# An attention and expert-routing kernel with its chunk loads relaid to 112 and 128 rows, quarter-tile scores and token-major outputs

## The chip, the cores and the metric

The kernel runs on one core of one Trainium2 chip. The metric is the device time in microseconds of one execution; what is shown is the median of three runs.

## The reference

An mLSTM (linear attention with exponential gates) feeds a mixture of experts that keeps the 80 best tokens of each expert.

```python
def _attn_ref(q, k, v, i_gate, f_gate, o_gate):      # B, H, S, D = 4, 8, 768, 40
    for t in range(S):
        m_new = np.maximum(f_gate[:, :, t] + m, i_gate[:, :, t])
        f_stab = np.exp(f_gate[:, :, t] + m - m_new)
        i_stab = np.exp(i_gate[:, :, t] - m_new)
        m = m_new
        C = f_stab * C + i_stab * outer(v[t], k[t])   # per batch and head, 40 x 40
        n = f_stab * n + i_stab * k[t]
        denom = np.maximum(np.abs(n @ q[t]), 1.0)
        y[t] = sigmoid(o_gate[t]) * (C @ q[t]) / denom

def _moe_ref(x, w_gate, w1, w2, capacity):            # 3072 tokens x 320, 8 experts, 1024 hidden
    expert_idx = argmax(x @ w_gate);  gate_w = softmax(x @ w_gate)[expert_idx]
    for e in range(E):
        tok_idx = tokens of e, at most the `capacity` (80) of largest gate_w
        out[tok_idx] = gate_w[tok_idx] * (relu(x[tok_idx] @ w1[e]) @ w2[e])
```

Tokens that no expert keeps stay zero in `out`.

## The kernel before, in words

The sequence is cut into 12 chunks of 64 steps (`NC`, `T`). The 32 pairs of batch and head are 16 groups of two; each chunk is done in two half chunks of eight groups, so there are 24 steps `i` (`NHS`), with chunk `c = i // 2` and half `hb = i % 2`. Within a chunk the recurrence is a masked score matrix; between chunks a 40 x 41 state is carried (`cs`, with a copy `cb` in the layout that the matmul wants). The stages of a step:

- `s_arg` (L371, L373): a matmul of `lh` and `rc` makes the logarithms of the decay in PSUM, and ACT's exp writes `w`. `lh` and `rc` hold gate sums that go through a DRAM tile (`d2`: `store_d2`, `load_lh`, `load_rc`).
- `s_s` (L398): scores S = K Q, eight matmuls that are each two records in the profile; `s_p` (L404): DVE multiplies S with `w` into `p`; `s_kw` (L388): POOL scales the keys.
- `s_int` (L424): the part from the carried state, in `hib`; `s_pv` (L412): `p` times V, in `h`; `s_st` (L433): the state update, in `cps`.
- `s_post` (L441 to L456): DVE puts the parts together, makes the reciprocal `rd` of the denominator and the product `u` with the output gate; POOL multiplies `u` and `rd` into `xn`.
- `s_state` (L483 to L493): DVE adds the update to the decayed state, and ACT copies it to `cb` in four pieces of 40 x 164. In three of the steps (`OFF`) DVE and POOL copy.
- `s_tp`, `s_xt` (L508, L523): PE transposes the finished 128 x 320 tile, ACT copies it out of PSUM; `s_z`, `s_lg` (L531, L545, L546) make the gating logits of a chunk by matmul, copy, transpose and reduction; `s_gate` picks the expert; `s_cmp` and `s_cnt` count gate values over thresholds; `s_xd` (L540) stores the finished chunk to DRAM.

Each chunk comes in by six loads from SP's queue: two of `qk` (40 rows each), two of `q2` (the queries in a second layout, 40 rows each) and two of `kv` (64 rows each), into two buffers (`NV = 2`). The rows of a buffer that no load fills are set to zero once, before the loop (`zeros`, `zero_v`).

The order on each engine is written out by hand. `PRE` lists the operations before the loop, `BODY` the stages of one step (run for i = 2 to 21), `TAIL` those after it; all DMAs in these lists are issued by SP in that order, so that a DMA that waits holds up those behind it.

In the loop SP also loads the output gates (`og` into `xn`), the weights of the first expert pair (`b_w`, four parts), and writes zeros over the whole output in four DMAs (`b_zero`, steps 9, 10, 17, 21).

After the loop and its tail, routing finds for each expert the 80 largest gates by three rounds of comparisons (L908 to L969), eight indirect DMAs gather the tokens, and the experts follow in four pairs (`f_h`, `f_o`), with weights streamed in behind; indirect DMAs scatter the result over the zeroed output.

Of the kernel before, what the change touches and what calls it, by code (L numbers as in the profile page):

```python
# [9 lines left out]
F32 = mybir.dt.float32  # L10
# [9 lines left out]
NP = 4  # L20
# [5 lines left out]
VN, KN = G16 * V1, G16 * D  # L26
E = 8
# [46 lines left out]
def tile_mlstm_moe(ctx, tc, cap, qk_d, q2_d, kv0_d, kv1_d, og_d, if_d, cst_d, cs2_d, zr_d, wz_d, w1_d, w2_d, out_d, dbg=None):  # L74
# [72 lines left out]
    zt = cp.tile([128, 480], F32, name="zt")  # L147
# [36 lines left out]
    A.activation(ez, zb[0:1, 0:1], AF.Exp)  # L184
# [144 lines left out]
    def store_d2(c0, c1):  # L329
        s, e = c0 * T, c1 * T  # L330
        SP.dma_start(d2[:, :, :, :, s:e].rearrange("k a g h t -> (g h) (k a) t"),
                     lb[:, :, :, s:e].rearrange("r k a t -> r (k a) t"))
# [58 lines left out]
    def s_s(i):  # L391
        c, hb = divmod(i, 2)
        qk = qk_b[c % NV]
        sp = ps.tile([128, 4, 2, T], F32, tag="s", name=f"s{i}")
        for q in range(4):
            for y in range(2):
                g = 8 * hb + 2 * q + y
                TE.matmul(sp[64 * y:64 * y + 64, q], lhsT=qk[:, 1, g], rhs=qk[:, 0:3:2, g], start=True, stop=True)  # L398
        pp = wk.tile([128, 8, T], F32, tag="p", name=f"p{i}")
        st["p", i] = (pp, sp.rearrange("r q x t -> r (q x) t"))  # L400

    def s_p(i):
        pp, sp = st["p", i]
        V.tensor_tensor(pp, sp, st.pop(("w", i)), ALU.mult)  # L404

    def s_pv(i):
        c, hb = divmod(i, 2)
        pp, _ = st.pop(("p", i))
        hp = (ps if i == NHS - 1 else ps1).tile([128, 4, 2, V1], F32, tag="s" if i == NHS - 1 else "h", name=f"h{i}")
        for p in range(8):  # L410
            r0 = 64 * (p % 2)
            TE.matmul(hp[r0:r0 + 64, p // 2], lhsT=pp[:, p], rhs=vb[c % NV][:, :, 8 * hb + p], start=True, stop=True)  # L412
        st["h", i] = hp

    def s_int(i):
# [3 lines left out]
        hi = ps1.tile([128, 512], F32, tag="ar", name="hil")[:, 0:8 * V1].rearrange("r (q y v) -> r q y v", y=2, v=V1) if i == NHS - 1 else hiv  # L419
        st["hi", i] = hi  # L420
        for p in range(8):
            g = 8 * hb + p
            r0 = 64 * (p % 2)
            TE.matmul(hi[r0:r0 + 64, p // 2], lhsT=q2_b[c % NV][:, g], rhs=cb[:, :, g], start=True, stop=True)  # L424
# [784 lines left out]
```

## Time and profile before

| | |
|---|---|
| runs | 265.21, 265.52, 266.19 us; median 265.52 |
| profiled execution | span 271.7 us (first to last instruction); no other time of it is given |
| PE, DVE, ACT, POOL busy in it | 222.0, 134.1, 92.3, 106.2 us |
| moved by DMA | 55.68 MB, mean 205 GB/s |
| mean granted TensorE clock | 0.858 |

An engine's busy time is a sum over stages with different limits. A row of a window gives for one stretch the busy time of PE, PEld (weight loads), DVE, ACT and POOL with the number of instructions, the granted TensorE clock as a share, the mean busy share of the 16 DMA engines, and GB/s. A row of the timeline gives start, length, engine, line, operation, output and inputs, and in brackets how long the engine was idle before and what ended that. KB are 1024 bytes, MB and GB powers of ten.

### The profile page before, as it was taken

What the parts mean: (1) busy time and instruction counts of PE and PEld (TensorE: products, weight loads), DVE (VectorE), ACT (ScalarE), POOL (GpSimd) and SP (SyncE); (2) the same over time, 40 slices, a digit from 0 to 9 for tenths busy, and PEclk for the clock granted to TensorE, in tenths of its full rate; (3) what the DMA queues carried; (4) which work ended last, traced back from release to release, by engine and by line L of the source; (5) the groups of instructions that cost most, each with busy time, mean ns of one, the idle gap of its engine ahead of it and who ended that gap; (6) DMA issues with size and microseconds to landing.
All of it is one profiled execution on the core that took longest, in us unless ns stands there. A gap on an engine that the chain in (4) does not pass through costs nothing. (4 is left out here: it accounts for less than half of the span.)

```text
span 271.7 us, 7189 instructions
## 1 busy us (share of the span) xinstructions
PE 222.0 (82%) x2938; PEld 164.7 (61%) x2938; DVE 134.1 (49%) x393; ACT 92.3 (34%) x215; POOL 106.2 (39%) x195
## 2 busy tenths in 40 slices
PE   6795999239746999799493889887897999999992
PEld 2364877128534977587382676656455896489640
DVE  8975989806741579789444488533700000100010
ACT  5465466537432955244333333200000121013100
POOL 9761766445545265666440831300047000111021
PEclk9999599759995799899869599865657699999998
DMA  5986479889889978979999965960012999980010
GB/s 125 192 223 173 156 195 276 170 195 224 229 201 281 231 237 232 215 211 186 331 208 215 257 193 135 421 291 0 2 32 76 364 420 420 422 372 24 0 39 23
DMA packets 21337, 55.68 MB, mean 205 GB/s; under 512 B 5000, under 2 KB 14024, under 8 KB 18552
## 3 DMA queue, kind: packets, MB, share of 16 engines
q1 hardware_dynamic: 20488, 53.33, 67.6%
q0 software_dynamic: 672, 1.64, 2.0%
q8 instruction: 23, 0.38, 0.6%
q10 hardware_dynamic: 144, 0.26, 0.3%
q14 instruction: 10, 0.08, 0.1%
HBM read 46.26 MB, written 9.12 MB: 204 GB/s over the span
## 5 line engine op out<-in xcount | busy, mean ns | idle before, releaser
L388 POOL TENSOR_TENSOR kw<-kv,w 128x320 f32<-128x320 f32 x22 | 16.7, 759 | 50.1 <-DMA kv<-in_kv 39.2
L398 PE MATMUL s<-qk 128*64 128x128 f32 x384 | 33.1, 327 | 2.2 <-DMA qk<-in_qk 0.8
L398 PEld LDWEIGHTS s<-qk 128*64 128x64 f32 x384 | 26.4, 166 | 10.9 <-issue 7.1
L493 ACT COPY cb<-cs 40x164 f32<-40x164 f32 x76 | 25.1, 330 | 11.0 <-DVE cs L483 8.9
L1025 PE MATMUL hp<-cx,w 128*64 128x80 f32 x512 | 25.6, 243 | 2.0 <-issue 1.6
L412 PE MATMUL h<-kv,p 128*64 128x82 f32 x384 | 20.2, 251 | 7.8 <-DMA kv<-in_kv 7.8
L1064 POOL DMA_INDIRECT out<-ob,iqi x6 | 5.9, 978 | 52.7 <-DVE ob L1061 36.0
L1057 PE MATMUL op<-w,ht 128*64 128x320 f32 (+1 forms) x256 | 26.4, 433 | 0.0
L1025 PEld LDWEIGHTS hp<-cx,w 128*64 128x64 f32 x512 | 24.3, 146 | 2.5 <-issue 1.8
L371 PE MATMUL ar<-rc,lh 118*128 118x512 bf16 x22 | 10.0, 456 | 18.2 <-DMA qk<-in_qk 9.2
L456 POOL TENSOR_TENSOR xn<-u,rd 128x320 f32<-128x320 f32 x23 | 17.3, 755 | 15.4 <-DVE u L455 14.3
L412 PEld LDWEIGHTS h<-kv,p 128*64 128x64 f32 x384 | 17.7, 150 | 8.8 <-issue 6.1
L441 DVE TENSOR_TENSOR hs<-hib,gn 128x328 f32<-128x328 f32 x21 | 10.3, 493 | 21.7 <-PE hib L424 21.7
L1057 PEld LDWEIGHTS op<-w,ht 128*64 128x64 f32 (+1 forms) x256 | 12.6, 117 | 12.8 <-issue 5.3
L373 ACT ACTIVATE w<-ar 128x512 f32<-128x512 f32 x22 | 13.1, 596 | 20.8 <-PE ar L371 20.0
L1061 DVE TENSOR_SCALAR ob<-op,iq 128x320 f32<-128x320 f32 (+1 forms) x6 | 3.1, 523 | 33.1 <-PE op L1057 33.1
L972 POOL DMA_INDIRECT xg<-xd,idx x8 | 7.9, 985 | 29.6 <-DVE gi L980 27.5
L523 ACT COPY xt<-tp 128x384 f32<-128x384 f32 x20 | 9.5, 479 | 29.4 <-PE tp L508 29.3
L424 PE MATMUL hib<-cb,q 128*64 128x82 f32 x336 | 17.9, 254 | 1.8 <-DMA q<-in_q 1.5
L433 PE MATMUL cps<-kv,kw 128*40 128x82 f32 x352 | 18.9, 255 | 0.0
L1044 ACT ACTIVATE ht<-hp 128x320 f32<-128x320 f32 x16 | 7.0, 437 | 34.5 <-PE hp L1025 34.5
L424 PEld LDWEIGHTS hib<-cb,q 128*64 128x64 f32 x336 | 16.4, 153 | 2.9 <-DVE p L404 1.1
(215 smaller groups left out, 415.7 us busy)
## 6 DMA issues: line engine op xcount, KB each, us to landing
w<-in_w SPq DMA_DIRECT2D x14, 1280.0 KB
kv<-in_kv SPq DMA_DIRECT2D x24, 324.0 KB
qk<-in_qk SPq DMA_DIRECT2D x24, 320.0 KB
xd<-xn SPq DMA_DIRECT2D x24, 160.0 KB
out<-zt SPq DMA_DIRECT2D x4, 960.0 KB
q<-in_q SPq DMA_DIRECT2D x22, 160.0 KB
xn<-in_og SPq DMA_DIRECT2D x9, 320.0 KB
w<-in_w SPq DMA_DIRECT2D x4, 640.0 KB
```

The source lines that it names most:

```text
L371: TE.matmul(ar, lhsT=lh[:, c].rearrange("r h t -> r (h t)"), rhs=rc[c // 2 % NRC][:, gs_(i), c % 2, :], start=True, stop=True)
L373: A.activation(w, ar, AF.Exp)
L388: P.tensor_tensor(kw, kn_b[c % NV][:, gs_(i)], st["w", i][:, :, T - 1:T].broadcast_to([128, 8, D]), ALU.mult)
L398: TE.matmul(sp[64 * y:64 * y + 64, q], lhsT=qk[:, 1, g], rhs=qk[:, 0:3:2, g], start=True, stop=True)
L412: TE.matmul(hp[r0:r0 + 64, p // 2], lhsT=pp[:, p], rhs=vb[c % NV][:, :, 8 * hb + p], start=True, stop=True)
L424: TE.matmul(hi[r0:r0 + 64, p // 2], lhsT=q2_b[c % NV][:, g], rhs=cb[:, :, g], start=True, stop=True)
L433: TE.matmul(cpv[r0:r0 + 40, p // 2], lhsT=kw[:, p], rhs=vb[c % NV][:, :, 8 * hb + p], start=True, stop=True)
L441: V.tensor_tensor(hs, st.pop(("hi", i)), gn[:, c, gs].rearrange("r (q a) -> r q a", a=2).unsqueeze(3).broadcast_to([128, 4, 2, V1]), ALU.mult)
L456: P.tensor_tensor(xn[:, i], u, rd.broadcast_to([128, 8, D]), ALU.mult)
L493: A.copy(dst, src)
L1025: TE.matmul(out, lhsT=w[:, k, c0:c0 + 64], rhs=rhs, start=start, stop=stop)
L1057: TE.matmul(o[gw * j:gw * j + m, 0:DM], lhsT=hts[p][:, f, a, t0:t0 + m], rhs=w[:, a, f], start=(f == 0), stop=(f == 7), tile_position=(0, ...
```

## The change

- *Loads.* One `qk` tile of 112 rows (q and k of one half of the groups in rows 0 to 39, of the other in rows 64 to 103, zeros between them written on the host) and one `kv` tile of 128 rows (values in a block layout with their zeros, and keys). `q2` and the zero fills go. Three buffers.
- *Scores.* S by 16 matmuls on quarters of the array (40 rows in, 64 out, 64 columns) into one PSUM tile of two banks.
- *Outputs.* Rows of `xn` are tokens with all heads in order; the store `xd` has rows of 1280 B instead of 640 B. `w_gate` and `w1` keep their order.
- *Logits.* `s_z` writes the logits of each half chunk to PSUM directly; the copy `zs`, its transpose and the reduction go.
- *Post.* One fused step for the absolute value, `u` on POOL, and the product with the clipped reciprocal on DVE (`s_fin`). The copies to `cb` are two of 40 x 328, always on ACT.
- *Order.* `gt` and `cst` are loaded in two parts; the first round trip of the gates through DRAM is issued by ACT; the output is zeroed after the loop, behind two weight tiles; the first weight tile is loaded in steps 18 to 21 instead of 15 on; sigmoids in four groups instead of three; gates chosen at other steps.

```diff
-BODY = "tab pr0 cmp s zero int pv tp st load xt xd cg p w post arg0 pr1 cnt pg z state d2 arg1 sig lh og lg"
+BODY = "tab pr0 cmp s int pv tp st load xt xd cg p w post arg0 pr1 cnt pg z state fin d2 arg1 sig lh og"
-PRE = "qb msk qa lq0 ad0 zv0 zc mkb wm lk0 al0 fl lo p0 p0 qc0 p0 ...
+PRE = "lq0 lgt lk0 lo0 lcb lq1 lk1 lo1 msk zc mkb wm ad0 al0 fl p0 p0 p0 p0 p1 p0 sig a0 brc p1 s0 ...
-    SP.dma_start(gt, if_d)
+    SP.dma_start(gt[:, :, 0:2 * T], if_d[:, :, 0:2 * T])
-    A.dma_start(cst, cst_d)
+    A.dma_start(cst[:, 0:CST_A], cst_d[:, 0:CST_A])
-    NV = 2
-    qk_b = [cp.tile([128, 3, G16, T], F32, name=f"qk{i}") for i in range(NV)]
-    q2_b = [cp.tile([128, G16, T], F32, name=f"q2{i}") for i in range(NV)]
-    kv_b = [cp.tile([128, 2, VN + KN], F32, name=f"kv{i}") for i in range(NV)]
+    NV = 3
+    qk_b = [cp.tile([QR, 2, G16, T], F32, name=f"qk{i}") for i in range(NV)]
+    kv_b = [cp.tile([128, KVN], F32, name=f"kv{i}") for i in range(NV)]
+    sps = ps1.tile([128, 2, 2, 4, T], F32, tag="s", name="sps")
     def load_qk(c):
-        SP.dma_start(qk_b[j][0:40, 0:2], qk_d[c, 0])
-        SP.dma_start(qk_b[j][64:104, 1:3], qk_d[c, 1])
+        SP.dma_start(qk_b[c % NV], qk_d[c])
     def load_kv(c):
-        SP.dma_start(kv_b[j][0:64, 0], kv0_d[c])
-        SP.dma_start(kv_b[j][64:128].rearrange("r y n -> r (y n)")[:, VN:2 * VN + KN], kv1_d[c])
+        SP.dma_start(kv_b[c % NV], kv_d[c])
     def s_s(i):
-        sp = ps.tile([128, 4, 2, T], F32, tag="s", name=f"s{i}")
+        sp = sps[:, :, hb]
         for q in range(4):
             for y in range(2):
-                TE.matmul(sp[64 * y:64 * y + 64, q], lhsT=qk[:, 1, g], rhs=qk[:, 0:3:2, g], start=True, stop=True)
+                for x in range(2):
+                    g = 8 * hb + 2 * q + y
+                    r = slice(64 * x, 64 * x + D)
+                    TE.matmul(sp[64 * y:64 * y + 64, x, q], lhsT=qk[r, 1, g], rhs=qk[r, 0, g], start=True, stop=True)
     def s_int(i):
-            TE.matmul(hi[r0:r0 + 64, p // 2], lhsT=q2_b[c % NV][:, g], rhs=cb[:, :, g], start=True, stop=True)
+                    TE.matmul(hi[64 * r:64 * r + 64, 2 * a:2 * a + 2, y], lhsT=qk_b[c % NV][0:104, 0, g], rhs=cb[:, g], start=True, stop=True)
     def s_post(i):
-        V.tensor_scalar(rd, hv[:, :, D:V1], -1.0, 1.0, ALU.mult, ALU.max)
-        V.tensor_tensor(rd, hv[:, :, D:V1], rd, ALU.max)
+        V.scalar_tensor_tensor(rd, hv[:, :, D:V1], -1.0, hv[:, :, D:V1], ALU.mult, ALU.max)
+        P.tensor_tensor(u, hv[:, :, 0:D], xn[:, i], ALU.mult)
         V.reciprocal(rd, rd)
-        (V if i < UV else P).tensor_tensor(u, hv[:, :, 0:D], xn[:, i], ALU.mult)
-        P.tensor_tensor(xn[:, i], u, rd.broadcast_to([128, 8, D]), ALU.mult)
+    def s_fin(i):
+        V.scalar_tensor_tensor(xn[:, i], rd.broadcast_to([128, 8, D]), 1.0, u, ALU.min, ALU.mult)
     def s_state(i):
-        for x in range(2):
-            for y in range(2):
-                ...
         for x in range(2):
+            r = slice(64 * x, 64 * x + D)
+            A.copy(cb[r, gs, x], cs[r, 4 * hb:4 * hb + 4].rearrange("r q y v -> r (q y) v"))
+    def s_z(i):
+        lgp = lga[:, i] if i < LG else st["lgb"][:, i - LG]
+        for k in range(3):
+            for r in range(2):
+                TE.matmul(lgp[64 * r:64 * r + 64], lhsT=xt[:, k, 64 * r:64 * r + 64], rhs=wz[:, k], start=(k == 0), stop=(k == 2))
-        sd1=lambda: store_d2(1, 2), lh1=lambda: load_lh(1, 2),
+        sd1=lambda: store_d2(1, 2, A), lh1=lambda: load_lh(1, 2, A),
-    def b_zero(i): ...
     for p_, kind, k in ((wp, 0, 1), (wq, 1, 0)):
         run(load_w(p_, kind, k))
+    for k in range(4):
+        SP.dma_start(out_d.rearrange("(p r) d -> p (r d)", p=128)[:, 1920 * k:1920 * (k + 1)].rearrange("p (r n) -> p r n", n=480),
+                     zt.unsqueeze(1).broadcast_to([128, 4, 480]))
```

More of the change, by code (lines that the diff above doesn't have):

```diff
@@ L192, in warmc @@
         for _ in range(n):
-            TE.matmul(cps, lhsT=zb[:, 0:128], rhs=zb, start=True, stop=True)
+            TE.matmul(sps[:, 0].rearrange("r h q t -> r (h q t)"), lhsT=zb[:, 0:128], rhs=zb, start=True, stop=True)
     def c2(name, rows=128):
@@ L509, in s_tp @@
         st["tp", i] = tp
[L510 removed]
     def s_xt(i):
[L513 to L516 removed]
+        xt = wk.tile([128, 3, 128], F32, tag="xt", name=f"xt{i}")
+        st["xt", i] = xt
         tp = st.pop(("tp", i))
[L518 removed]
+        if i == NHS - 1:
             V.tensor_copy(xt[:, 0:XL], tp[:, 0:XL])
[L520 to L523 removed]
@@ L525, in s_z @@
-    def s_z(c):
-        st["zx"] = st["x"]
-        xt = st.pop(("xt", c))
-        for k in (0, 1, 2):
-            for x in range(2):
-                j = 2 * x + (k == 1)
-                TE.matmul(st["zx"][32 * j:32 * j + 32], lhsT=wz[:, x, k], rhs=xt[:, k, :, 64 * x:64 * x + 64],
-                          start=(k < 2), stop=(k > 0), tile_position=(0, 32 * j))
-        zs = wk.tile([128, 128], F32, tag="zs", name=f"zs{c}")
-        A.copy(zs, st["zx"])
-        st["zs", c] = zs
-    def s_xd(c):
-        i = 2 * c + 1
-        for eo in range(2):
-            SP.dma_start(
-                xd.rearrange("(b s) e f -> s b e f", b=B)[c * T:(c + 1) * T, :, eo],
-                xn[64 * eo:64 * eo + 64, i - 1:i + 1].rearrange("t h (b p) d -> t (h b) (p d)", b=2))
@@ L544, in s_lg @@
-    def s_lg(c):
-        TE.transpose(st["zx"], st.pop(("zs", c)), ident)
-        V.tensor_reduce(lg[:, c].rearrange("r a e -> r (a e)"), st["zx"].rearrange("r (j e) -> r e j", j=4)[:, 0:2 * E], AX.X, ALU.add)
-    def s_gate(c0, c1, lv=None):
+            A.copy(xt[:, XL:3], tp[:, XL:3])
+        else:
+            A.copy(xt, tp)
+    def s_z(i):
+        xt = st.pop(("xt", i))
+        if i == LG:
+            st["lgb"] = ps1.tile([128, 2, E], F32, tag="h", name="lgb")
+        lgp = lga[:, i] if i < LG else st["lgb"][:, i - LG]
+        for k in range(3):
+            for r in range(2):
+                TE.matmul(lgp[64 * r:64 * r + 64], lhsT=xt[:, k, 64 * r:64 * r + 64], rhs=wz[:, k], start=(k == 0), stop=(k == 2))
@@ L549, in s_gate @@
+    def s_xd(c):
+        for r in range(2):
+            SP.dma_start(xd.rearrange("(b r s) f -> r s b f", r=2, s=S)[r, c * T:(c + 1) * T],
+                         xn[64 * r:64 * r + 64, 2 * c:2 * c + 2].rearrange("t b h d -> t b (h d)"))
+    def s_gate(c0, c1):
         n = c1 - c0
         sh = [128, 2 * n, E]
-        lv = lg[:, c0:c1].rearrange("r c a e -> r (c a) e") if lv is None else lv
+        lv = lga[:, 2 * c0:2 * c1] if c1 < NC else st["lgb"]
         gv = gate[:, c0:c1].rearrange("r c a -> r (c a)")
@@ L615, in s_cnt @@
             V.tensor_tensor(ncnt, ncnt, cpc, ALU.subtract)
-    def s_zl(hb):
-        if hb == 0:
-            st["zl"] = ps1.tile([128, 2, E], F32, tag="h", name="zl")
-        xt = st["xt", NC - 1][:, :, hb]
-        for k in (0, 1, 2):
-            for x in range(2):
-                TE.matmul(st["zl"][64 * hb:64 * hb + 64], lhsT=xt[:, k, 64 * x:64 * x + 64],
-                          rhs=wz[:, x, k, 0:2 * E], start=(k == 0 and x == 0), stop=(k == 2 and x == 1))
     def s_sig(i):
@@ L714, in b_xt @@
     def b_xt(i):
-        if i >= 3 and i not in OFF:
+        if i >= 3:
             s_xt(i - 1)
@@ L738, in b_z @@
     def b_z(i):
-        if i >= 3 and i % 2 == 1:
-            s_z((i - 3) // 2)
+        if i == 2:
+            s_z(0)
+        s_z(i - 1)
     def b_cmp(i):
@@ L1158, in by_x @@
         return six(a).transpose(4, 2, 6, 0, 1, 3, 5).reshape(NC, 2, D, G16, T)
-    def by_y(a):
-        return six(a).transpose(4, 3, 6, 0, 1, 2, 5).reshape(NC, 2, D, G16, T)
     def nat(a):
```

268 lines of the change are left out of this document (104 added, 164 removed).

## The prediction

> **What bounds the kernel now.** I read the stages first (windows of the span: busy time of each engine, granted TensorE clock, DMA share, GB/s), cut at the first inter-chunk matmul (29.60), at that of iteration 22, the first after the loop (159.4), at the start of routing (171.4) and at the expert matmuls (207).
>
> ```profile
> 0.00:29.60 29.60, 22.49 (x166) 13.11 (x166) 23.16 (x68) 17.15 (x26) 18.62 (x23) 0.96 0.76 180
> 29.60:159.40 129.80, 100.46 (x1559) 80.85 (x1558) 82.66 (x229) 60.70 (x149) 68.81 (x144) 0.84 0.88 224
> 159.40:171.40 12.00, 10.67 (x151) 7.88 (x150) 9.91 (x47) 5.13 (x16) 3.73 (x7) 1.00 0.58 176
> 171.40:207.00 35.60, 30.79 (x165) 20.28 (x166) 13.33 (x41) 0.39 (x2) 6.58 (x9) 0.66 0.34 132
> ```
>
> The columns are PE, PEld, DVE, ACT, POOL, clock, DMA share, GB/s. The second row is half the span: 20 loop iterations, 6.49 us each. No compute engine fills it (PE 100.5 of 129.8, at a mean clock of 0.84), but the DMA engines are busy 0.88 of it at only 224 GB/s. Next, the waits of that stretch (total, times, longest):
>
> ```profile
> POOL kw L388 <- DMA kv<-in_kv: 36.4, 6, 10.8
> ...
> DVE hs L441 <- PE hib L424: 21.7, 11, 9.1
> ```
>
> Six waits for `kv` stand at the head; the PE and DVE waits behind them are their echo. Then the rate of each kind of transfer, in windows in which nearly nothing else moves (64-row `kv`; 40-row `qk`; zeroing of the output from 128 rows; `xd` stores; 128-row expert weights):
>
> ```profile
> 21.00:23.00 2.00, 1.41 (x34) 1.25 (x31) 1.90 (x10) 1.95 (x5) 0.02 (x1) 1.00 0.59 135
> 28.00:31.80 3.80, 3.80 (x44) 3.22 (x45) 3.77 (x10) 2.24 (x9) 3.38 (x6) 0.50 0.61 213
> 85.50:88.00 2.50, 2.50 (x23) 1.53 (x23) 0.87 (x2) 1.01 (x5) 1.23 (x2) 0.50 1.05 397
> 167.00:168.00 1.00, 1.00 (x21) 0.87 (x20) 0.63 (x5) 0.25 (x2) 0.00 (x0) 1.00 0.94 234
> 223.00:233.00 10.00, 10.00 (x126) 6.74 (x124) 1.11 (x3) 1.31 (x4) 1.01 (x1) 1.00 1.01 420
> ```
>
> Loads of 40 or 64 rows leave 0.4 of the DMA engines idle even alone, and move 135 to 213 GB/s; 128-row transfers fill them and move 397 to 420. So the loop is bound by how its loads are shaped. What would the loop cost without that? The inter-chunk matmuls (16 records an iteration) count iterations:
>
> ```profile
> 29.60:42.90 13.30, 2.10 (x32) 1.79 (x32) 0.82 0.69 183
> 61.60:75.20 13.60, 2.21 (x48) 2.02 (x50) 1.00 0.91 228
> 89.30:108.70 19.40, 3.52 (x64) 3.20 (x64) 0.92 0.86 232
> 116.10:128.85 12.75, 2.21 (x48) 2.04 (x48) 1.00 0.86 195
> ```
>
> The last three hold 3 + 4 + 3 iterations in 45.75 us: 4.58 each, where data are nearly in time. The first two iterations take 13.3, laden with the gate scans. The PE timeline of a quiet iteration shows its pace:
>
> ```profile
> 102.68 0.33 PE L545 MATMUL tp<-cst,zs 128*128 128x128 f32 x1
> 102.94 1.09 PE L398 MATMUL s<-qk 128*64 128x128 f32 x16
> 103.86 0.74 PE L424 MATMUL hib<-cb,q 128*64 128x82 f32 x16
> 104.43 0.74 PE L412 MATMUL h<-kv,p 128*64 128x82 f32 x16
> 105.09 0.55 PE L508 MATMUL tp<-cst,xn 128*128 128x128 f32 x3
> 105.57 0.77 PE L433 MATMUL cps<-kv,kw 128*40 128x82 f32 x16
> 106.27 0.63 PE L531 MATMUL tp<-xt,wz 128*32 128x128 f32 x12
> 106.83 0.39 PE L371 MATMUL ar<-rc,lh 118*128 118x512 bf16 x1
> 107.15 0.44 PE L398 MATMUL s<-qk 128*64 128x128 f32 x4
> ```
>
> From S (102.94) to the next S (107.15) is 4.21 us without a gap: behind the DMA stands PE.
>
> **The change part by part.** The sum is made against the profiled execution (span 271.7; the page gives no other time of it); the median of the runs is 265.52, so 6.2 go off at the end.
>
> ```profile
> kv<-in_kv SPq DMA_DIRECT2D x24, 324.0 KB
> qk<-in_qk SPq DMA_DIRECT2D x24, 320.0 KB
> xd<-xn SPq DMA_DIRECT2D x24, 160.0 KB
> out<-zt SPq DMA_DIRECT2D x4, 960.0 KB
> q<-in_q SPq DMA_DIRECT2D x22, 160.0 KB
> ```
>
> *Loads.* A chunk (two iterations) now takes 2x324 + 2x320 + 2x160 = 1608 KB in six issues. By the shapes in the diff it becomes 128 x 1952 x 4 B = 976 KB of `kv` and 112 x 2048 x 4 B = 896 KB of `qk` in two issues: 1872 KB, 264 more, padding included. At 420 GB/s that is 4.56 us. With 320 KB of `og` at 397 (0.83) and 320 KB of `xd` at 234 (1.40) a chunk costs 6.8 us of transfer in the 9.2 that two iterations take. So DMA drops from the bound to 74%; bounds 6.8 (these rows) and, if the new loads stay at 224 GB/s, 11.5. I take the first, since 128 rows are the shape of the 420 row; 112 rows are nearer to it than to 64. A third buffer lets a load start about 2.5 iterations (11 us) before its first use, against some 5 us of transfer.
>
> *Zeroing.* 4 x 960 KB = 3.93 MB leave the loop: 9.9 us of DMA at 397 GB/s, inside what is counted above. It is queued on SP behind two weight tiles (5.2 MB, 12.5 us at 420) after the loop. The cover is routing: 35.6 us at a DMA share of 0.34, that is 12.1 busy; 22 of 35.6 after. The next SP instruction behind it is the store of the indices, at the end of routing. Cost 0; without the cover, 9.9.
>
> *PE.* S goes from 16 records of 128 columns to 32 of 64 columns on quarter tiles. In the timeline S takes 0.92 start to start (57 ns a record of 128 columns), L424 0.57 (36 ns, 82 columns). Extended to 64 columns: 27 ns, 32 x 27 = 0.87. If four quarters overlap, half of it, 0.43. Unoverlapped small records are these 24, 1.4 us in all, 57 ns each:
>
> ```profile
> L493 ACT COPY cb<-cs 40x164 f32<-40x164 f32 x76 | 25.1, 330 | 11.0 <-DVE cs L483 8.9 <-DVE cs L485 0.6
> ...
> L523 ACT COPY xt<-tp 128x384 f32<-128x384 f32 x20 | 9.5, 479 | 29.4 <-PE tp L508 29.3
> ...
> L623 PE MATMUL zl<-wz,xt 128*64 128x16 f32 x24 | 1.4, 211 | 0.0
> ```
>
> That gives 1.8. I take 0.92, no change; range -0.5 to +0.9 an iteration. S loses its separate PSUM buffers (the halves now share banks): S of i+2 must follow the product `p` of i, which DVE was given an iteration earlier, and 0 is taken for it. The Trainium skill, TensorEngine Tiling (Array Packing), section Performance Considerations, says that a matmul costs some 60 cycles however few its columns are, and that a tiling factor should not be taken from a dimension already small. It also says (Tiling Modes) that a change of tiling mode drains the array. It speaks against quarter tiles: at 2.4 GHz, an estimate of 25 ns x 32 = 0.8 and two drains more an iteration. By it the sum moves by less than 2 us.
>
> Logits change from 12 records every second iteration plus a transpose (0.56 + 0.26 over two, 0.41) to 12 records each iteration, 0.32 to 0.68 by the same two prices: +0.1. Inter-chunk, PV and state matmuls keep count and width.
>
> *ACT, DVE, POOL.* The state copies become 2 of 328 elements for 4 of 164: between the two ACT rows 0.68 ns an element, so 0.44 each, 0.88 for 1.32. The zs copy goes, so ACT gains some 0.5 an iteration, in idle time: 0 on the path. DVE trades `u` for the fused min-multiply (same size) and loses one of two small steps and the logit reduction; POOL trades the `xn` product for `u`. Both stay below PE (82.7 and 68.8 us for 20 iterations now, 4.1 and 3.4 each), so 0. One new order: `xn` now waits for POOL's `u`, then DVE; its reader, the transpose, stands 3 us into the next PE iteration.
>
> Loop: 18 x (4.58 + 0.1) = 84.2, the first two 13.3, rest waits 1.5: 99. It is 129.8 now: -30.8.
>
> *Before the loop.* The zero fills go, the gate inputs and constants are split so the scans start sooner, and the gates' round trip through DRAM goes to ACT's queue:
>
> ```profile
> 5.78 0.28 DVE L297 TENSOR_TENSOR_SCAN m<-gt 32x64 f32<-32x64 f32 x1
> ...
> 12.90 0.34 SPq L331 DMA_DIRECT2D d<-lb  x1
> ...
> 25.76 0.38 PE L371 MATMUL ar<-rc,lh 118*128 118x512 bf16 x1 [2.34 <-DMA rc<-d]
> ```
>
> Store to matmul is 12.9 us, with bulk loads queued between on SP. The scans can start some 3 us sooner, and the trip can shrink by 5 or more; against that, four DMAs are issued by ACT, which stands still until the store has landed, with the first state copies and the exp of iteration 2 behind it (DVE and PE wait for these), and the first sigmoid, ahead of the first exp, now waits for its `og`. SP, rid of them, issues the loads of chunks 2 and 3 sooner. Bounds -9 and +3; I take -6. *Behind the loop:* a few small DVE steps and two transposes of the 0.26 kind less, -0.5 (bounds -1.5, +2). Routing and experts: the same work, 0.
>
> Sum: -30.8 - 6 - 0.5 = -37.3: span 234.4, runs 228.
>
> **The rivals.** *A2, serial quarters:* S costs 1.8 instead of 0.92, 20 x 0.88 = +18 on a loop that PE paces: 246. For it: 57 ns at L623; against: those 24 write one half of the PSUM rows, then the other; S's 32 alternate over four quarters.
>
> *B, the byte rate stays:* the padded loads move no faster than 224 GB/s. Ten chunks of 1872 + 640 KB and a weight tile (2560 KB) are 28.3 MB, 126 us: loop -3.5, with the prologue -6 and -0.5 behind: 255.5. For it: `xd` and 64-row traffic interleave with everything; against: 397 and 420 in two windows. Forecast and B part at 28.3 MB / 99 us = 286 GB/s. The Trainium skill (SBUF — State Buffer, section on door 1, the DMA port swizzle) says that DMA bandwidth depends on how many of 16 ports the rows reach, and that 64 adjoining rows reach half. By that rule 112 and 128 rows are freed, and 4.56 us a chunk holds; the 135 and 213 GB/s rows agree.
>
> *C, nothing moves:* as B, and ACT's wait for the round trip costs the 3 of its bound instead of giving 6: -3.5 + 3 - 0.5 = -1, 264.5. For it: ACT also carries the exps; against: they wait for the same trip today.
>
> *D, slower:* gaps between small matmuls make the granted clock fall to half inside S (0.50 is seen in the 28.0 window), with no quarters overlapping: 32 x 114 ns = 3.65 for S, 7.4 an iteration, loop 18 x 7.4 + 14.8 = 148, +18 - 6.5 = +11.7: 277. It decides from S = 3.0 on (loop 136, then 18 iterations of 6.75). Against it: in the quiet stretches without gaps the clock is 0.92 to 1.00.
>
> **How the numbers follow.** Chances: forecast 0.70 (own range 215 to 239), A2 0.12, B 0.11, C 0.03, D 0.04. The forecast's range is the prologue (-9 to +3) and +-0.35 on 18 iterations with S between its rows. For 8 in 10 the range reaches to A2 and leaves out B, C and D, 0.18: 213 to 247. Below 213 PE's 4.21 floor for 20 iterations would have to hold with the whole -9. About 0.5% (1.3 us) is what a measurement of this kernel can tell from no change. Faster: forecast, A2 and B, 0.93; same: C, 0.03; slower: D, 0.04.
>
> **What would show it.** Right: DMA share in the loop near 0.75 at 280 to 310 GB/s, waits for `kv` under 5 us, iterations of 4.5 to 5.0, granted clock near 1.0, zeroing wholly inside routing, first inter-chunk matmul near 23.6. Wrong: S over 1.2 us start to start (A2), DMA share still 0.88 or more at 224 (B), routing longer than 36 us (zeroing not covered), the first inter-chunk matmul at 29 or later.

## Result and the profile after

The change made the kernel faster by a quarter of what was forecast: 257.4 us (median of 4 runs, 255.0 to 260.4) against 265.9 of before beside it, a ratio of 0.962 (95% interval 0.953 to 0.972); the forecast was 228. Two later comparisons of the same two kernels gave 0.976 (0.963 to 0.990) and 0.960 (0.953 to 0.968). The profile shown is of the longest of the four runs (260.4); two more profiles of the changed kernel, e9 and e21, stand beside it where it matters. Ratios compare the runs within 1.5% of each kernel's fastest, so they can differ from the quotient of the medians, and of the three profiles of the changed kernel only e9's is of such a run.

First the stages (windows of the span, columns as before: PE, PEld, DVE, ACT, POOL, clock, DMA share, GB/s), cut at the first inter-chunk matmul, at that of iteration 22, at the first routing step, at the first slot matmul of routing and at the end:

```profile
0.00:26.58 26.58, 17.02 (x230) 9.66 (x230) 17.81 (x60) 9.52 (x17) 8.20 (x15) 0.81 0.79 246
26.58:147.45 120.87, 99.11 (x2000) 80.99 (x2000) 82.99 (x193) 61.01 (x122) 71.63 (x137) 0.80 0.74 230
147.45:164.10 16.65, 14.33 (x154) 9.70 (x151) 10.66 (x46) 3.76 (x11) 3.82 (x8) 0.69 0.57 194
```

The DMA share of the loop fell from 0.88 to 0.74, as forecast, yet the loop is 120.9 us long and not 99. The waits of that stretch (total, times, longest) no longer name `kv` at all:

```profile
DVE cs L460 <- PE cps L500: 16.7, 12, 5.7
...
PE cps L500 <- ACT xt L491: 7.3, 2, 3.8
...
PE tp L480 <- DVE xn L435: 4.5, 4, 1.8
PE cps L500 <- DMA wz<-in_wz: 4.5, 1, 4.5
```

L500 is the gate matmul `s_z`, L491 ACT's copy `xt`, L435 the new fused product on DVE, L460 the state addition. PE waits for two small copies, 7.3 us, and once for the 12 KB of `wz`. In a quiet iteration nothing waits (PE timeline, start and length):

```profile
118.01 0.69 PE L368 MATMUL sps<-qk 40*64 40x64 f32 x32
118.63 0.79 PE L400 MATMUL hib<-cb,qk 104*64 104x82 f32 x16
119.25 0.74 PE L387 MATMUL h<-kv,p 128*64 128x82 f32 x16
119.93 0.55 PE L480 MATMUL tp<-cst,xn 128*128 128x128 f32 x3
120.41 0.77 PE L409 MATMUL cps<-kv,kw 128*40 128x82 f32 x16
121.11 0.39 PE L339 MATMUL ar<-rc,lh 118*128 118x512 bf16 x1
121.43 0.52 PE L500 MATMUL cps<-wz,xt 128*64 128x8 f32 x12
121.88 0.69 PE L368 MATMUL sps<-qk 40*64 40x64 f32 x32
```

From S to S 3.87 us without a gap: better than the forecast's 4.68. S itself takes 0.62 start to start, 0.92 before. So PE bounds a quiet iteration, and the time is lost in the long ones. The starts of the inter-chunk matmuls of iterations 2 to 22 are apart by 15.3, 8.4, 5.7, 3.9, 9.5, 4.8, 4.1, 6.0, 4.5, 5.6, 4.5, 9.7, 6.2, 3.9, 3.9, 7.8, 5.6, 3.9, 3.9, 3.8 us. The one of 9.5 (59.8 to 69.3), on PE and on ACT:

```profile
62.42 0.77 PE L409 MATMUL cps<-kv,kw 128*40 128x82 f32 x16
66.97 0.82 PE L500 MATMUL cps<-wz,xt 128*64 128x8 f32 x12 [3.79 <-ACT xt L491]
67.72 0.61 PE L339 MATMUL ar<-rc,lh 118*128 118x512 bf16 x1
68.26 1.13 PE L368 MATMUL sps<-qk 40*64 40x64 f32 x32
69.33 1.36 PE L400 MATMUL hib<-cb,qk 104*64 104x82 f32 x16
```

```profile
60.92 1.28 ACT L579 ACT_TABLE_LOAD   x1
62.22 2.43 ACT L579 ACTIVATE xn<-xn 128x640 f32<-128x640 f32 x2
64.65 1.28 ACT L580 ACT_TABLE_LOAD   x1
65.95 0.20 ACT L580 ACTIVATE ez<-zb 1x1 f32<-1x1 bf16 x1
66.06 0.49 ACT L290 CAST lb<-rb 32x384 bf16<-32x384 f32 x1
66.46 0.46 ACT L491 COPY xt<-tp 128x384 f32<-128x384 f32 x1
```

The copy stands behind a sigmoid group with its two table loads, 5.2 us; PE stands behind the copy; and after the pause every matmul takes nearly twice its time (S 1.13, inter-chunk 1.36), since the granted clock fell:

```profile
60.00:64.00 4.00, 2.40 (x51) 1.88 (x47) 3.66 (x8) 3.95 (x5) 2.51 (x4) 1.00 0.97 304
64.00:68.00 4.00, 1.03 (x13) 0.83 (x13) 1.29 (x7) 3.04 (x6) 2.19 (x4) 0.57 0.70 274
68.00:72.00 4.00, 4.00 (x68) 3.40 (x67) 3.91 (x7) 1.53 (x3) 1.59 (x3) 0.58 0.33 64
72.00:76.00 4.00, 4.00 (x100) 3.27 (x100) 3.33 (x8) 2.32 (x5) 3.30 (x12) 1.00 0.89 279
```

The theory that the experiments test: the loads are off the path; PE paces the loop, and in-order waits that lay unseen under the waits for `kv` now stop it, each dearer by the half-clock time behind it (*pause theory*). Rivals: the loop still hangs on when loads land (*load theory*); a pause costs only its own length; the late zeroing did it.

### The profile page after: what moved, and what is told of

The parts are those of the page before. It is cut to its first block, busy times and chain, and to the rows that moved or that the text cites. A ratio compares the mean times of both kernels' runs of the same rounds, so it can differ in the third digit from the quotient of the medians.

```text
span 258.5 us, 8067 instructions
## 1 busy us (share of the span) xinstructions
PE 214.7 (83%) x3443; PEld 161.8 (63%) x3443; DVE 129.1 (50%) x347; ACT 84.3 (33%) x175; POOL 97.7 (38%) x177
## 5 line engine op out<-in xcount | busy, mean ns | idle before, releaser
L428 POOL TENSOR_TENSOR u<-hs,xn 128x320 f32<-128x320 f32 x23 | 18.7, 812 | 39.4 <-DVE hs L419 20.8
L465 ACT COPY cb<-cs 40x328 f32<-40x328 f32 x44 | 20.6, 468 | 33.7 <-DVE cs L460 25.5
L985 PE MATMUL op<-w,ht 128*64 128x320 f32 (+1 forms) x256 | 26.5, 433 | 0.0
L500 PE MATMUL cps<-wz,xt 128*64 128x8 f32 x264 | 13.1, 219 | 14.9 <-ACT xt L491 7.5
L368 PE MATMUL sps<-qk 40*64 40x64 f32 x768 | 19.7, 251 | 4.7 <-DVE p L376 4.7
L356 POOL TENSOR_TENSOR kw<-kv,w 128x320 f32<-128x320 f32 x22 | 17.2, 782 | 16.0 <-ACT w L349 9.2
L500 PEld LDWEIGHTS cps<-wz,xt 128*64 128x64 f32 x264 | 11.3, 160 | 18.3 <-ACT xt L491 9.9
L368 PEld LDWEIGHTS sps<-qk 40*64 40x64 f32 x768 | 16.1, 158 | 9.7 <-DVE p L376 5.7
L400 PE MATMUL hib<-cb,qk 104*64 104x82 f32 x336 | 20.1, 269 | 0.8 <-issue 0.8
L480 PE MATMUL tp<-cst,xn 128*128 128x128 f32 x72 | 15.1, 328 | 6.3 <-DVE xn L435 4.5
L900 POOL DMA_INDIRECT xg<-xd,idx x8 | 7.9, 982 | 31.6 <-DVE gi L908 29.4
L376 DVE TENSOR_TENSOR p<-sps,w 128x512 f32<-128x512 f32 x24 | 16.4, 682 | 6.7 <-ACT w L341 4.2
L387 PEld LDWEIGHTS h<-kv,p 128*64 128x64 f32 x368 | 18.8, 166 | 1.3 <-issue 1.1
L491 ACT COPY xt<-tp 128x384 f32<-128x384 f32 x23 | 11.0, 478 | 25.9 <-PE tp L480 25.9
L435 DVE SCALAR_TENSOR_TENSOR xn<-rd,u 128x320 f32<-128x320 f32 x23 | 18.5, 806 | 1.1 <-POOL u L428 0.7
```

Source lines behind the costliest of these rows:

```text
L356: P.tensor_tensor(kw, kn_b[c % NV][:, gs_(i)], st["w", i][:, :, T - 1:T].broadcast_to([128, 8, D]), ALU.mult)
L368: TE.matmul(sp[64 * y:64 * y + 64, x, q], lhsT=qk[r, 1, g], rhs=qk[r, 0, g], start=True, stop=True)
L376: V.tensor_tensor(by_x(st["p", i]), sps[:, :, i % 2], by_x(st.pop(("w", i))), ALU.mult)
L387: TE.matmul(hp[64 * r:64 * r + 64, p], lhsT=pp[:, 4 * r + p], rhs=vb[c % NV][:, 8 * hb + 4 * r + p], start=True, stop=True)
L400: TE.matmul(hi[64 * r:64 * r + 64, 2 * a:2 * a + 2, y], lhsT=qk_b[c % NV][0:104, 0, g], rhs=cb[:, g], start=True, stop=True)
L428: P.tensor_tensor(u, hv[:, :, 0:D], xn[:, i], ALU.mult)
```

## The experiments

All by stages, in us, from each one's profile: to the first inter-chunk matmul, the first two iterations, the other 18, from iteration 22 to the first routing step, and from the first slot matmul to the end. Time is the median of all runs, with that of before beside it. For e7, e11, e14, e17 and e18 no ratio is on record. On record only the changed kernel (the first comparison and e21), e19 and e20 count as clearly faster than before; for the others the stages carry the argument.

| kernel | start | first 2 | other 18 | behind | last stage | time / before |
|---|---|---|---|---|---|---|
| before | 29.6 | 13.4 | 116.4 | 12.0 | 76.5 | |
| e14, before again | 31.1 | 12.6 | 115.2 | 12.1 | 77.1 | 274.9 / 274.0 |
| changed | 26.6 | 23.6 | 97.2 | 16.5 | 71.0 | 257.4 / 265.9 |
| e9, changed again | 28.9 | 19.1 | 94.5 | 14.1 | 70.7 | 254.4 / 265.4 |
| e21, changed again | 28.3 | 18.8 | 101.4 | 14.0 | 70.8 | 256.1 / 266.0 |
| e5, no loads in the loop | 29.4 | 18.5 | 93.4 | 13.9 | 77.5 | 258.6 / 271.7 |
| e12, zeroing in the loop | 27.7 | 20.5 | 95.5 | 15.4 | 76.8 | 262.5 / 274.0 |
| e1, `wz` early | 26.4 | 17.1 | 94.1 | 16.3 | 76.6 | 259.1 / 271.7 |
| e3, gate matmuls later | 27.4 | 18.4 | 85.6 | 16.4 | 76.8 | 253.3 / 271.7 |
| e7, copies off ACT | 27.5 | 20.7 | 87.8 | 16.5 | 71.0 | 250.9 / 265.4 |
| e4, fillers in two pauses | 28.0 | 20.3 | 91.7 | 15.3 | 76.7 | 257.6 / 271.7 |
| e2, `u` and product as before | 27.5 | 21.0 | 92.0 | 15.7 | 69.9 | 253.5 / 265.4 |
| e8, sigmoids ahead merged | 32.5 | 12.3 | 102.0 | 16.5 | 69.9 | 257.6 / 265.4 |
| e11, store ahead of loads | 28.2 | 20.5 | 96.9 | 15.0 | 78.9 | 264.7 / 274.0 |
| e16, one load later | 26.9 | 25.4 | 96.2 | 15.0 | 69.8 | 259.0 / 265.8 |
| e17, fillers behind out | 29.1 | 18.6 | 96.5 | 12.5 | 70.5 | 255.4 / 265.8 |
| e13, combined | 27.5 | 17.6 | 87.8 | 16.6 | 76.8 | 250.0 / 274.0 |
| e18, combined, fillers out | 26.7 | 17.2 | 92.4 | 13.5 | 71.2 | 245.4 / 265.8 |
| e19, e18 with dense fillers | 27.5 | 16.2 | 89.5 | 13.8 | 70.2 | 243.9 / 265.8 |
| e20, as e18 | 26.9 | 17.2 | 84.6 | 16.2 | 70.1 | 240.2 / 266.0 |

**A measure first.** The last stage is 70 to 71 or 77 to 79 us, and before itself takes 271.7 to 274.0 where it is long and 265.4 to 266.0 where it is short.

> The kernel before, unedited, for a second profile of it by the same cuts: to the first inter-chunk matmul 29.6, loop 129.8, then 35.8 to the first slot matmul of routing and 76.5 from there to the end in the profile shown. If the last stage belongs to the chip and not to the kernel, it is 70 to 71 here wherever the changed kernel's is; the loop, if the first profile was an ordinary one, is 125 to 131.

> The changed kernel once more, unedited, so that the edits beside it have their measure on the same chip: 0.962 of the time of before (0.953 to 0.972).

The second profile of before has 127.8 in the loop, 77.1 in the last stage, beside 76.8 to 78.9 of the three other kernels run with it. All kernels of one comparison ran on one chip, and the last stage goes with the comparison. So the 5.5 us that the last stage seems to lose between the two profiles first compared is not the change; only ratios within one comparison, and the other stages, are read from here on. e9 gave 0.976, above its expected 0.962 but with an interval that reaches down to 0.963.

The other stages have a spread too: the 18 iterations of the changed kernel took 94.5, 97.2 and 101.4 us in its three profiles, and those of e18 and e20, which are one kernel, 92.4 and 84.6. A difference of a few us in that column shows nothing by itself. Single iterations repeat better. Iterations 6 and 13, in which PE pauses, and 7 and 14 behind them take 30.2, 30.9 and 30.9 us together in the three profiles of the changed kernel. The edits at these pauses are read by this sum.

**Are the loads off the path?** e5 issues no load of `qk` and `kv` in the loop, so its iterations compute on old chunks:

```diff
-            if c + NV < NC:
+            if c + NV < 0:
                 load_qk(c + NV)
```

> The loads of qk and kv for chunks 3 and later that the loop issues are left out (iterations compute on the chunk that the buffer still holds). Pause theory: the loads are off the path, 0 to 4 us less than the changed kernel, the same pauses at the same places. Load theory: the loop falls by 15 us or more.

```profile
29.40:141.30 111.90, 95.07 (x2002) 77.59 (x2002) 77.49 (x190) 59.59 (x121) 71.67 (x134) 0.84 0.35 104
```

The DMA share of the loop falls from 0.74 to 0.35; the loop is 111.9 us, 113.6 in e9. Ratio 0.961 (0.953 to 0.969), that of the changed kernel. The load theory, by which the loop would have fallen by 15 us or more, is out.

**The late zeroing.** e12 puts the four stores back into iterations 9, 10, 17 and 21.

> The zeroing of the output goes back into the loop, to iterations 9, 10, 17 and 21 as before. Pause theory: the loop no longer waits for loads, so 9.9 us more of DMA in it cost 0 to 3 us, and routing is shorter by 0 to 2: 0 to 3 us more than the changed kernel, or none. If the late zeroing was what made the change faster: 8 to 10 more.

Ratio 0.966 (0.951 to 0.981), loop 116.0 at a DMA share of 0.82: no difference from the changed kernel (0.960 to 0.976) that these runs resolve. So the late zeroing is not what made the change faster; putting the stores back should then have cost 8 to 10 us.

**The wait for `wz`.**

```diff
-PRE = "... lo0 lcb lq1 ... lo3 lc2 w3 lz llt ..."
+PRE = "... lo0 lcb lz lq1 ... lo3 lc2 w3 llt ..."
```

> Only the place of the wz load in SP's queue changes (from behind the loads of chunk 3 and the constants to right behind the first chunk's). Pause theory: the gate matmuls of token block 0 no longer stand 4.47 us for wz at 34.9, the state addition behind them no longer waits 5.69, and some of the half-clock stretch behind it (40.8 to 53) goes too: 5 us less than the changed kernel (3 to 9), about 252. Load theory (the loop is still limited by when the bulk loads land): the time is given back at the next load, 0 to 1 us less.

The wait is gone and the first two iterations take 17.1 us, against 19.1 in e9, 18.8 in e21 and 23.6 in the profile shown; the ratio, 0.961 (0.943 to 0.980), doesn't resolve it. Some 2 us of that stage, more where the wait was longer.

**The copies behind the sigmoids.** Before, `OFF` gave `xt` and the state copies to DVE and POOL in the iteration behind a sigmoid; the change dropped it. e7 puts it back, for iterations 6 and 13 (there `xt` also moves behind `post`, and the counting that follows the gate step moves with it):

```diff
-            A.copy(cb[r, gs, x], cs[r, ...])
+            (A.copy if i not in OFF else (V, P)[x].tensor_copy)(cb[r, gs, x], cs[r, ...])
-            A.copy(xt, tp)
+            (V.tensor_copy if i + 1 in OFF else A.copy)(xt, tp)
-GATE = {6: (0, 2), ...
+GATE = {7: (0, 2), ...
```

> One thing that the change took away is put back: in the iteration behind each sigmoid group (6 and 13) the copy xt and the state copies cb are made by DVE and POOL and not by ACT, and the first gate step moves from iteration 6 to 7. Pause theory: PE's waits of 3.8 and 3.5 us for xt go, and with each an iteration at half clock: 10 us less than the changed kernel (6 to 14). If ACT's queue is not what makes these pauses: 0.

e3 leaves ACT alone and issues the gate matmuls an iteration later:

```diff
-BODY = "... int pv tp st load ... cnt pg z state ..."
+BODY = "... int pv z tp st load ... cnt pg state ..."
-        s_z(i - 1)
+        s_z(i - 2)
```

> The gate matmuls of a block are issued one iteration later, behind PV, so that PE does not stand in front of ACT's copy xt and the state addition does not stand behind the gate matmuls in their PSUM bank. Pause theory: the pauses of 4.5 (wz), 3.8 and 3.5 us (sigmoid on ACT ahead of xt) go, and with each most of one iteration at half clock (8.4 instead of 3.9): 16 us less than the changed kernel (8 to 22), about 241. If a pause costs only its own length: 11 to 12 less. Load theory: 0 to 4 less, with waits for qk and kv instead.

In e7 the iterations behind the sigmoids take 6.5 and 4.4 us instead of 9.6 and 9.7, and the sum of the four is 21.8 instead of 30.9 (e9, same comparison); in e3 it is 24.7, and e3's ratio is 0.942 (0.931 to 0.954). In e13, e18 and e20, which have both edits, it is 16.6 to 16.8. The cause stands, but each alone gave less in time than forecast: 3.5 us in e7's median, some 5 by e3's ratio. In e3 one pause moved on: in iteration 7 the gate step on DVE waits for ACT's exp, the state addition waits behind that, and PE waits 3.4 us for the addition.

**What a pause costs beside its length.** e4 leaves the pauses and fills them:

```diff
+            warmh(26)      # iterations 6 and 13, ahead of the gate matmuls
```

> 26 matmuls of zeros (328 columns, bf16, into bank hib) are added ahead of the gate matmuls in iterations 6 and 13, where PE stands 3.8 and 3.5 us for xt; the pauses themselves stay. Clock theory (a pause of that length halves the granted clock, and the iteration behind it runs at 8.4 instead of 3.9): 6 us less than the changed kernel (3 to 9), about 251, with the clock at 1.0 behind both places. If the clock is not what makes the pauses dear: 0, or up to 1 us more.

The iterations behind the two pauses take 4.1 and 4.5 us instead of 5.2 and 6.4 (e9), the pauses' own 9.2 and 8.7 instead of 9.6 and 9.7, and the clock is 1.00 in all four. So the half clock behind these pauses is real, and worth some 4 us over the two (26.5 for 30.9), where 6 were expected. The ratio, 0.957 (0.947 to 0.967), agrees with either.

**The fused product on DVE.** DVE's row of a quiet iteration, and one with POOL's products beside it:

```profile
118.61 0.48 DVE L435 SCALAR_TENSOR_TENSOR xn<-rd,u 128x320 f32<-128x320 f32 x1
...
123.48 2.09 DVE L435 SCALAR_TENSOR_TENSOR xn<-rd,u 128x320 f32<-128x320 f32 x1
```

```profile
123.80 0.73 POOL L471 TENSOR_TENSOR cg<-cs,gl 104x328 f32<-104x328 f32 x1
124.49 0.73 POOL L356 TENSOR_TENSOR kw<-kv,w 128x320 f32<-128x320 f32 x1
```

DVE's instruction ends (125.57) 0.35 us behind POOL's second (125.22). The Trainium skill, SBUF — State Buffer, section Who interferes with whom, says that a DVE instruction with two SBUF inputs contends with a GpSimd one that reads SBUF. Five of the 23 rows of L435 take 1.5 to 2.1 us, all beside `cg` and `kw`; the trace agrees. It isn't every time the DVE step that pays: at 83.92 it took 0.48 beside `kw` alone, and `kw` 1.18 instead of 0.73. e2 gives `u` to DVE and the product to POOL, as before:

```diff
-        P.tensor_tensor(u, hv[:, :, 0:D], xn[:, i], ALU.mult)
+        V.tensor_tensor(u, hv[:, :, 0:D], xn[:, i], ALU.mult)
+        P.tensor_tensor(xn[:, i], u, rd.broadcast_to([128, 8, D]), ALU.mult)
     def s_fin(i):
-        V.scalar_tensor_tensor(xn[:, i], rd.broadcast_to([128, 8, D]), 1.0, u, ALU.min, ALU.mult)
```

> The last steps of a token block go back to the engines of before: u on DVE, the product into xn on POOL (three small DVE steps as before in place of two). Port theory (the fused DVE step takes 1.8 to 2.1 us instead of 0.48 when POOL runs its two products beside it): DVE's part of it falls from a mean of 0.8 us to 0.45, 3 us less than the changed kernel (0 to 6). If the order of DVE's and POOL's work costs no time on the path: 0 (1 either way).

```profile
L430 DVE TENSOR_TENSOR u<-hs,xn 128x320 f32<-128x320 f32 x23 | 10.7, 464 | 0.0
...
L431 POOL TENSOR_TENSOR xn<-u,rd 128x320 f32<-128x320 f32 x23 | 20.8, 905 | 45.9 <-DVE u L430 41.6 <-DVE vf L558 3.4 <-DVE ncnt L574 0.9
```

DVE's mean falls as expected (806 to 464 ns), and PE's waits for `xn` from 3.9 us (e9) to 1.2; the time does not resolve it (0.974, 0.956 to 0.992, beside 0.976 for e9). Contention shown, its worth in time not.

**The start.** Three attempts to shorten the gates' round trip, three misses.

```diff
-SIG = {-2: (0, 2), -1: (2, 6), ...      # e8, and sig behind a0, a1 and sd1
+SIG = {-2: (0, 2, 6), ...
-... lcb lq1 lk1 lo1 msk ... sd1 k0      # e11, and the store on SP
+... lcb msk ... sd1 lq1 lk1 lo1 k0
-... p2 lq2 p2 a2 ... sd lk2             # e16
+... p2 p2 a2 ... sd lq2 lk2
```

> Ahead of the loop the two sigmoid groups become one, issued behind the first two exps and the gates' store on ACT: two table loads fewer, the first exp no longer behind the wait of 6.9 us for og, and no sigmoid at the first inter-chunk matmul. Pause theory: the first inter-chunk matmul 2 us sooner (1 to 4), the first iteration of the loop 4 us shorter (2 to 5): 5 us less than the changed kernel (2 to 8). If the gates' round trip through DRAM alone sets the start: 0 to 3 less, all of it in the first iteration.

> The loads of chunk 1 (qk, kv and og, 2.5 MB) move from ahead of the gates' store to behind it, and the store goes back to SP's queue. If the round trip through DRAM (11.5 to 25.5) is long because the bulk loads are ahead of it in the 16 DMA engines: the store lands some 5 us sooner, and the first inter-chunk matmul comes 2 us sooner (1 to 5), 2 us less than the changed kernel. If it is long because ACT waits in front of its loads: less than 1 us.

> One load (qk of chunk 2, 0.9 MB) moves behind the gates' second store. DMA theory (the start is set by the bytes ahead of the gates' round trip): the rows rc land sooner and the first inter-chunk matmul comes 2 us sooner (1 to 3.5), 2 us less than the changed kernel. ACT theory (ACT's wait for og and for the store sets it): 0 to 0.5.

e8: the merged sigmoid waits for its `og` until 21.0, and the loads of `lh` stand behind it on ACT; the first inter-chunk matmul comes at 32.5. The first two iterations are then 12.3. That is not the sigmoid group alone: the loop began 3.6 us later than in e9, and PE's wait for `wz` in it is 0.5 us instead of 3.7. Nothing is won in all. e11 shows the trip (store, then the load that waits for it; e9 and e11):

```profile
12.44 0.34 ACTq L299 DMA_DIRECT2D d<-lb  x1
20.11 0.68 ACTq L304 DMA_DIRECT2D lh<-d  x1
```

```profile
10.15 0.34 SPq L299 DMA_DIRECT2D d<-lb  x1
12.62 0.68 ACTq L304 DMA_DIRECT2D lh<-d  x1
15.89 1.99 ACTq L600 DMA_DIRECT2D rc<-d  x2
24.72 0.38 PE L339 MATMUL ar<-rc,lh 118*128 118x512 bf16 x1 [2.49 <-DMA rc<-d]
```

With the loads of chunk 1 behind it the store is followed by its load in 2.5 us instead of 7.7; but then the loads `rc` stand behind those 2.5 MB and PE still waits for them until 24.7. In e9 the store went from ACT's queue, away from the chunk loads on SP's, and took longer than in e11, where it went from SP's ahead of them; so here another queue did not help a small transfer past the bulk data. e16 took a load out that was behind, not ahead: the start did not move, and its first iteration waited 7.4 us for `wz` instead of 3.7 to 4.5.

**Behind the loop.** e17 sets `TW = [0, 0, 9, 4]` to `[0, 0, 2, 0]`.

> 11 of the 13 filler matmuls behind the loop are left out. If they hold up the last counts: from the inter-chunk matmul of iteration 22 to the first routing step 12 us instead of 14 to 16.5, 3 us less than the changed kernel (2 to 4). If the longer stage comes from the gate steps: 0, or up to 2 more where routing then runs at the lower clock.

12.5 us to the first routing step instead of 14.0 to 16.5, but routing then takes 24.8 for 23.6, and e18 and e20, without the same fillers, take 13.5 and 16.2. So the fillers are not shown to be the cause. Between profiles of one kernel the length of this stage goes with the granted clock: 1.00 in both of before (12.0 and 12.1 us); 0.88 in e9 and e21 (14.1 and 14.0) and 0.69 in the profile shown (16.5); 0.86 in e18 (13.5) and 0.62 in e20 (16.2).

**Together.** e13 is e1, e3 and e7; e18 and e20 are e13 with the fillers behind the loop left out; e19 adds `warmh(10)` and `warmh(8)` at the end of iterations 2 and 3.

> Three edits together: wz loaded early, the copies behind the sigmoid groups on DVE and POOL (first gate step in iteration 7), the gate matmuls one iteration later. Pause theory: the first two iterations 16 instead of 19 to 24, no PE wait for xt or wz over 1 us, the loop 98 to 102 instead of 113 to 121: 13 us less than the changed kernel (10 to 17). If the pauses move on to other waits: 5 to 8 less.

> The three edits of the combined kernel (wz early, copies behind the sigmoids on DVE and POOL, gate matmuls an iteration later) and the filler matmuls left out: 2 to 4 us below the combined kernel, 0.90 of before (0.88 to 0.92).

> As the one beside it, with 10 and 8 dense filler matmuls (328 columns, bf16, zeros) at the end of iterations 2 and 3, 1.1 to 2.7 us each. If dense matmuls bring the clock back, iterations 3 to 6 run at 4 to 5 us instead of 6 to 9: 4 us less (0 to 8). If they do not: 3 to 5 us more.

> The changed kernel once more, unedited, beside the combined one: 0.97 of before (0.95 to 0.99).

> The combined kernel with the filler matmuls left out, once more on one chip with the changed kernel. If the four places account for half of what the forecast missed: 0.91 of before (0.89 to 0.93), 12 to 18 us below the changed kernel. If they only move the pauses: 4 to 8 us below it.

```profile
26.90:128.80 101.90, 94.69 (x1991) 78.58 (x1991) 76.59 (x188) 57.80 (x115) 76.21 (x138) 0.83 0.85 271
```

Side by side in e20 and e21: 0.900 (0.894 to 0.907) against 0.960 (0.953 to 0.968), 240.2 us against 256.1, and a loop of 101.9 where 99 was forecast. e13 gave 0.905 (0.884 to 0.926), e19 0.915 (0.906 to 0.923). In e19 iterations 2 to 5 take 25.4 us, fillers included, and 27.3 to 29.2 in e13, e18 and e20; in the time (243.9, and 245.4 in e18 beside it) that is not resolved.

What is left is less waiting than clock. The 18 iterations of e9, e21, e18 and e20, columns as before:

```profile
47.96:142.45 94.49, 79.56 (x1756) 64.73 (x1750) 69.47 (x173) 50.63 (x98) 61.18 (x120) 0.91 0.73 233
47.07:148.50 101.43, 86.46 (x1756) 70.35 (x1750) 67.25 (x173) 50.60 (x98) 59.74 (x120) 0.83 0.68 217
43.93:136.36 92.43, 84.89 (x1753) 70.94 (x1751) 64.72 (x166) 46.02 (x89) 64.01 (x121) 0.82 0.76 245
44.18:128.78 84.60, 78.97 (x1753) 65.99 (x1751) 64.30 (x166) 46.15 (x89) 64.64 (x121) 0.88 0.83 266
```

PE's idle time, length less busy, is 14.9 and 15.0 us in the two profiles of the changed kernel and 7.5 and 5.6 in the two of the combined one. Within the pairs it differs by 0.1 and 1.9 us, and the lengths by 6.9 and 7.8: what differs is mostly how long the matmuls take, and with it the clock. In e20 two stretches, 35.4 to 50.8 and 69.2 to 82.9, run at 0.50 and 0.55 with PE busy throughout.

## Why the prediction was wrong

*Right.* The loads: DMA share 0.74, no wait for `kv`, and no gain left in them that e5 resolves. The zeroing at 0, as far as e12 resolves it. Rival A2 is out: S 0.62 start to start, 32 records at 19 ns, below the forecast's 0.92 and below the 27 ns that it drew from the rows without overlap, so some of the work on the quarters seems to overlap. That is also less than the estimate of 0.8 worked out from the Trainium skill's 60 cycles a matmul (TensorEngine Tiling (Array Packing), Performance Considerations). Rival B came within 2 us of the time by luck, not by its mechanism: the byte rate did not bind, and e20's loop moves 271 GB/s. D's half clock did appear, behind pauses and in stretches without one, not from gaps inside S.

*The step that failed* is the loop's sum, "18 x (4.58 + 0.1) = 84.2, the first two 13.3, rest waits 1.5: 99". The terms against the three profiles of the changed kernel:

- Pace: 3.9 and not 4.68, 14 us better over 18 iterations. S gave 0.3 an iteration of it. Much of the rest is that 4.58 was no quiet pace but a mean over iterations of 3.8 to 5.6 us, with waits in it.
- "Rest waits 1.5": the 18 iterations took 94.5 to 101.4 where 84.2 and 1.5 were forecast; above 18 x 3.9 = 70.2 that is 24 to 31. This is the term that was mis-sized. In e9 PE is idle for 14.9 us of it; the other 9.4 are mostly matmuls at the lower clock.
- Within it an item was left out: I counted the copies' length ("ACT gains some 0.5 an iteration, in idle time: 0") and not that without `OFF` they stand behind the sigmoids, with PE's gate matmul behind them. It is worth 9 us at the four iterations by e7 and 14 with e3's edit added; some 4 of it are the half clock (e4).
- Once those and `wz` are mended, 84.6 us (e20) or 92.4 (e18) are left, 14 or 22 above 70.2. PE is idle for only 5.6 or 7.5 of that; most of the rest goes with the half clock. What holds the clock down with PE busy stays open.
- "The first two 13.3": 18.8 to 23.6. Left out: `wz`, queued behind the loads of chunk 3 (17.1 without the wait, e1). The second sigmoid group ahead of the loop may be another part; e8 does not separate it from its later start. The clock is a third: 0.63 and 0.73 in e9's iterations 2 and 3, 0.82 before.
- "Fused min-multiply (same size)": 0.81 us mean for 0.46 (e2). The size was wrong; what it costs on the path is not resolved.
- "Granted clock near 1.0": 0.80, 0.87 and 0.79 over this loop in its three profiles, and 0.84 before.

That e20's loop comes near the forecast's 99 is in part luck: its pace is 0.8 better, and its clock costs what the sum did not have.

*Before the loop* -6 was taken; the start came 1 to 4 us sooner. The trip through DRAM didn't shrink (store to first matmul 12.9 before, 12.1 in e9): what it waits for are bytes ahead of it in the DMA engines, as e11 shows for the store. The bound of +3 named ACT's wait for `og` rightly (6.9 us on ACT) and still took -6.

*Behind the loop* -0.5 was taken; it was 14.0 to 16.5 for 12.0, at a granted clock of 0.69 to 0.88 for 1.00. Why the clock is lower there is open; e17 and e20 together do not make it the fillers.

The stages add up: start -2.5, first two +7.5, the others -18, behind +3, routing -1 from the means of two and three profiles, -11 in all; the medians say -8.5 to -11. The last stage is left out, as said.

## What to carry to other kernels

When the bound of a loop is taken away, its next pace is not the quiet iteration but the sum over all iterations, and waits that are covered today must be listed one by one: what stands in front of each engine's queue in the iterations that differ (table loads, gate steps, first use of a small constant). A diff that drops a special case (`OFF`) removes the answer to a wait that somebody met; ask which one. A pause on PE was paid twice here, by its length and by the half clock behind it. And before an edit is priced from one stage of one profile, a second profile of the same kernel shows how far that stage moves by itself: 7 to 8 us here.

## What was not expected of the hardware

The clock can stay at half without a gap on PE. In e13 (4 us windows) PE is busy throughout from 32 to 52, at a granted clock of 0.50 until about 50, with DMA at 0.40 to 0.99:

```profile
32.00:36.00 4.00, 4.00 (x51) 2.86 (x55) 3.40 (x9) 2.09 (x6) 2.19 (x3) 0.50 0.99 382
...
44.00:48.00 4.00, 4.00 (x77) 3.85 (x76) 2.58 (x4) 1.96 (x4) 0.18 (x1) 0.50 0.98 329
48.00:52.00 4.00, 4.00 (x80) 3.17 (x81) 2.98 (x8) 1.96 (x5) 2.40 (x3) 0.75 0.40 120
52.00:56.00 4.00, 4.00 (x112) 3.40 (x108) 2.40 (x6) 2.93 (x7) 3.94 (x10) 1.00 0.79 227
```

The Trainium skill (TensorE: Matmul & The Clock Gate, Part 1) gives some 3.4 us of sustained work for the full clock; behind the pause that ended at 67.0 in the changed kernel it took 4.4, here some 18 (from a gap of 0.9 us that ended at 31.9). What tells them apart is open. In all these traces the half clock comes in whole steps of 3.41 us: each of the 173 stretches that begin and end inside a span lasts 3.41, 6.83, 10.24 us and so on, up to 37.55.

In e13 PE also stopped in the middle of a group of matmuls, for nothing that the profile names:

```profile
116.92 0.59 PE L388 MATMUL h<-kv,p 128*64 128x82 f32 x10
120.67 0.43 PE L388 MATMUL h<-kv,p 128*64 128x82 f32 x5 [3.16 <-issue]
```

From 116 to 120 the DMA engines were busy 1.02 at 396 GB/s with weights, and a 16 KB packet of the instruction queue (`q8`) ran from 118.13 to 119.23. A second such stop, 1.47 us from 70.4, has one from 69.45 to 70.55. The other traces settle more: between 25 and 160 us of all profiles there are 19 stops of over 1 us that the profile puts down to `issue` (one in e14, the kernel before), and each ends 1.2 to 1.6 us behind the end of such a packet, though the packets come only every 4 to 10 us in this loop. That PE waited for its instructions there is the only reading that I see, but no run changed the packets. Such a stop falls in another place in each profile, and e4's (2.4 us) cost its iteration 20 some 4 us, half clock included.
